# Batch 1's loads in another order, an earlier gate, and seven filler products in the opening of a Fourier-plus-channel-mix kernel

## The chip, the cores and the metric

The kernel runs on one core of one Trainium2 chip. The metric is device time in microseconds (us) of one execution. Three runs of the kernel before took 435.13, 437.23 and 437.72 us; the median is 437.23.

## The reference

```python
X = np.fft.fft(x, axis=1); X = np.fft.fft(X, axis=2); x = X.real   # x: (8, 3072, 256)
x_prev = concat([zeros, x[:, :-1, :]], axis=1)
xk = mu_k * x + (1 - mu_k) * x_prev
xr = mu_r * x + (1 - mu_r) * x_prev
k = np.maximum(xk @ w_k, 0)          # 256 -> 1024
v = (k * k) @ w_v                    # 1024 -> 256
out = sigmoid(xr @ w_r) * v
```

Eight batches of 3072 rows of 256 numbers go through the real part of a two-dimensional Fourier transform, then through a channel mix with a shift by one row.

## The kernel before, in words

The Fourier transform is a chain of small matrix products per batch. `load_xh(b, h)` loads one half (h = 0 or 1) of batch b: rows in order into `xp` (`load_p`, a plain DMA), and mirrored rows into `xm` (`load_m`, an indirect DMA over an index list; for half 0 also a small one, `load_m0`). `fold` (VectorE, L168 and L170) adds the two. The a stage (`a_sum`, `a_item`, L574 and others) multiplies by a cosine and sine table into PSUM, from where it is copied to the tile `a`; the d stage (`d_units`, L596, evicted by `d_evac` at L511 or L513) gives `g_all`; the c stage (`c_sums`, L637) gives `y`. `diff` and the mixes on VectorE turn `y` into the shifted mixes `x_t[b, 0, m]` (for w_k) and `x_t[b, 1, m]` (for w_r), where m is one of the two halves of the sequence.

The channel mix works on 48 chunks of 512 rows, three to each half of a batch. A chunk has four steps; at each step `k_piece` makes two 128-column groups of x times w_k (L748), which ScalarE evicts with a Relu (L758) and VectorE or ScalarE squares (L768, L766). `r_item` (L775, evicted with a Sigmoid at L780) makes the gate r. `v_part` (L801) and `v_tile` (L789) multiply the squares by w_v into two PSUM buffers, and `v_out` (VectorE, L811) multiplies by r and stores the rows with DMAs from the SP queue.

All instructions are in a fixed order on each engine (`pin_order`), the order in which the program writes them: an opening written out by hand, up to the first products with w_k, and then a table of steps (`at`, `event`). A blocked instruction blocks everything behind it on its engine. For instance `at(4, fold, 1, 0)` puts the fold of batch 1, half 0 into VectorE's order at step 4, ahead of that step's square.

All loads of x and of the weights w_k, w_r and w_v go through POOL's queue, in its order. POOL uses eight completion semaphores in turn, so each of its DMAs is issued only when the one eight before it has landed. `load_gate` holds POOL back until VectorE has reached a given place: VectorE clears a one-element tile with a memset (L451), and POOL writes the same tile with an iota (L452), which must wait for that. `loads_1` opens with this gate and then gathers w_r for the first half of the channel mix (`wr_sb[0]`) and loads both halves of batch 1. `loads_2`, at step 4 of the table, makes new index lists and gathers w_k and w_r for the second half (`wk_sb[1]`, `wr_sb[1]`).

`keep_busy(n, ps, cols)` (L203) puts n products of a tile of zeros into TensorE's order; nothing reads their result. The tuple `NF` holds the counts for places in the opening. `NF[0]`, nine products into the PSUM tile `fill`, stands ahead of the small products for the mu columns (L834 and L330); `NF[3]`, three, ahead of the first d stage.

Of the kernel before, what the change touches and what calls it, by code (L numbers as in the profile page):

```python
# [20 lines left out]
def _v(ap, extra_offset, free_dims):  # L21
    new_ap = [list(ap.ap[0])] + [[s, c] for (s, c) in free_dims]
    return dataclasses.replace(ap, offset=ap.offset + extra_offset, ap=new_ap)
# [16 lines left out]
def kernel(  # L40
# [37 lines left out]
    def ps_w():  # L78
        return ps_slot("W", 3, 1024)

    def ps_v():
        return ps_slot("V", 2, 512)
# [35 lines left out]
    def x_tiles(b, h):  # L118
        xp_t[b, h] = xp_sb[(2 * b + h - 1) % 3] if b or h else xp_00
        xm_t[b, h] = xm_sb[(2 * b + h) % 3]  # L120
# [3 lines left out]
    def parts(b):  # L124
        return 112 if b > 1 else 96

    def load_p(b, h):
        r, n = 9 * h, 9 - h
        if b > 1:
            for g in range(2):  # L130
                src = dataclasses.replace(x[b, 32 * g + r:32 * g + r + 1, :],
                                          ap=[[64 * D, N1], [D, n], [1, D]])
                nc.gpsimd.dma_start(out=xp_t[b, h][64 * g:64 * g + N1, 0:n], in_=src)
            return
        src = dataclasses.replace(x[b, r:r + 1, :], ap=[[32 * D, 96], [D, n], [1, D]])
        nc.gpsimd.dma_start(out=xp_t[b, h][0:96, 0:n], in_=src)

    def gather(dst, src, idx):
        nc.gpsimd.indirect_dma_start(dst, None, src, bass.IndirectOffsetOnAxis(ap=idx, axis=0))  # L139

    def load_m(b, h, o, n, idx):
        gather(xm_t[b, h][0:parts(b), XM0 + o:XM0 + o + 256 * n],
               x.rearrange("b (s r) d -> (b s) (r d)", r=n), idx)

    def load_m0(b):
        if b == 0:
            gather(xm_00[:, 1:257], x.rearrange("b s d -> (b s) d"), idx_0[:, 0:1])
        else:
            load_m(b, 0, 2048, 1, (idx_g0 if b > 1 else idx_0)[:, b:b + 1])

    def load_xh(b, h):
        x_tiles(b, h)
        load_p(b, h)
        if h == 0:
            load_m0(b)
        load_m(b, h, 0, 8, (idx_g8 if b > 1 else idx_8)[:, b, h:h + 1])

    def fold(b, h, q0=0, n=0):

        n = n or 9 - h  # L160
        if (b, h) not in p_t:
            p_t[b, h] = p_pool.tile([112, 9, 256], FP16, name="p")
        k = parts(b)
        p, xp, xm = p_t[b, h][0:k], xp_t[b, h][0:k], xm_t[b, h][0:k]
        o = XM0 + 256 * (8 - h - q0)
        if (b, h, q0) == (0, 0, 0):
            xm, o = xm_00, 1
        V.tensor_tensor(out=p[:, q0:q0 + n], in0=xp[:, q0:q0 + n],  # L168
                        in1=_v(xm, o + 256, [(-256, n), (-1, 256)]), op=ALU.add)
        V.tensor_tensor(out=p[:, q0:q0 + n, 0], in0=xp[:, q0:q0 + n, 0],  # L170
                        in1=_v(xm, o, [(-256, n)]), op=ALU.add)
# [28 lines left out]
    def keep_busy(n, ps, cols=512):  # L200

        for _ in range(n):
            nc.tensor.matmul(out=ps[:, 0:cols], lhsT=zeros,  # L203
                             rhs=_v(zeros, 0, [(0, cols // P), (1, P)]), start=True, stop=True)

    fill = ps_w()
    keep_busy(4, fill)
    NF = (9, 0, 0, 3, 0, 3, 0)


    mu_row = const.tile([2, 256], FP32)
# [49 lines left out]
    def ts(out, in0, s1, op0, s2=None, op1=None):  # L261
        kw = {} if op1 is None else {"op1": op1}
        V.tensor_scalar(out=out, in0=in0, scalar1=s1, scalar2=s2, op0=op0, **kw)
# [17 lines left out]
    def rv(n, o, *dims, k=1):  # L281
        return _v(rw_0[0:k], P * n + o, list(dims)) if n < 6 else _v(rw_1, P * (n - 6) + o, list(dims))
# [45 lines left out]
    def outer(out, *pairs):  # L328
        for n, (row, r) in enumerate(pairs):
            nc.tensor.matmul(out=out, lhsT=row, rhs=r, start=n == 0, stop=n == len(pairs) - 1)  # L330
# [45 lines left out]
    ang_ps = [ps_v(), ps_v()]  # L376
# [31 lines left out]
    ts(ueo, ueo, TURN - 1, ALU.bitwise_and)  # L408
    keep_busy(NF[0], fill)

# [12 lines left out]
    def rows():  # L423
        for a in range(2):
            for half in range(2):
                iota(_v(row_i[64 * half:64 * half + 64], a, [(3 - 2 * a, 2)]), pattern=[[0, 2]],
                     base=256 * a + half * (1 - 2 * a), channel_multiplier=2 - 4 * a)
        iota(row_i[0:1, 2:3], pattern=[[0, 1]], base=0, channel_multiplier=0)
        iota(_v(row_i[0:1], 1, [(2, 2)]), pattern=[[0, 2]], base=128, channel_multiplier=0)
# [11 lines left out]
    def loads():  # L441
        rows()
        for a in range(2):
            gather(wk_sb[0][a], moe_w_k, row_i[:, a:a + 1])
        nc.gpsimd.dma_start(out=wv_sb, in_=moe_w_v.rearrange("(fc p) v -> p fc v", p=128))
# [4 lines left out]
    def load_gate():  # L450
        V.memset(gate, 0)  # L451
        iota(gate, pattern=[[0, 1]], base=0, channel_multiplier=0)  # L452

    def loads_1():
        load_gate()
        for a in range(2):
            gather(wr_sb[0][a], moe_w_r, row_i[:, a:a + 1])
        load_xh(1, 0)
        load_xh(1, 1)

    def loads_2():
        for lo in (0, 64):
            k = slice(lo, 64 if lo == 0 else 112)
            iota(idx_g8[k], pattern=[[S // 8, B], [-1, 2]], base=S // 8 - 1 - lo // 16,
                 channel_multiplier=-8)
            iota(idx_g0[k], pattern=[[S, B]], base=S - lo // 2, channel_multiplier=-64)
        iota(idx_g0[0:1], pattern=[[S, B]], base=0, channel_multiplier=0)
        for a in range(2):
            gather(wk_sb[1][a], moe_w_k, row_i[:, 2 + a:3 + a])
        for a in range(2):  # L470
            gather(wr_sb[1][a], moe_w_r, row_i[:, 2 + a:3 + a])

# [42 lines left out]
    def a_tile(b):  # L515
        a_t[b] = y_pool.tile([P, 2, NU, 64], FP16, name="a")
# [45 lines left out]
    def a_sum(b, h, i0, eng="A", m=4):  # L562


        if (h, i0) == (0, 0):
            a_tile(b)
        ps = ps_w() if m == 4 else ps_v()
        for i in range(m):
            parts = [(h, i0 + i + 1 - h, 0, 2 * WA, 0, 1)]
            if h and i0 + i == 7:  # L570
                parts = [(0, 0, 0, WA, WA, 1), (1, 7, 1, WA, 1, 2)]
            for half, q, o, n, w, step in parts:
                for k in range(2):
                    nc.tensor.matmul(out=_v(ps, 256 * i + o, [(2 * WA // n, n)]),  # L574
                                     lhsT=p_t[b, half][0:96, q, 128 * k:128 * k + 128],
                                     rhs=_v(w_pm[0:96], (WA + WB) * k + w,
                                            [(WA + WB, 2), (step, n // 2)]),
                                     start=(k == 0), stop=(k == 1))
        a_ps[b, h, i0] = ps
        if eng:  # L580
            a_evac(b, h, i0, eng, m)
# [3 lines left out]
    def a_evac(b, h, i0, eng, m=4):  # L585
        evac(_v(a_t[b], 8 * h + i0, [(16, 2 * WA), (1, m)]),
             _v(a_ps[b, h, i0], 0, [(1, 2 * WA), (256, m)]), eng)
# [12 lines left out]
    def d_evac(ps, u0, n, bank, eng):  # L600
        evac(_v(g_all, 256 * u0, [(64, 2), (128, 2 * n), (1, 64)]),
             _v(ps, 0, [(bank, 2), (64, 2 * n), (1, 64)]), eng)
# [234 lines left out]
        outer(mu_ps[:, 4 + n:5 + n], (tv(TO + n, 0, (1, P)), rv(ONE, 0, (1, 1))))  # L837
    for k in range(2):
        outer(mu_ps[:, 64 + NU * k:64 + NU * k + NU], (rw_h[:, k], rv(JR, 0, (1, NU))))
    a_sum(0, 0, 0)  # L840
    fold(0, 0, 5, 4)
    a_sum(0, 0, 4)
    half_tables(mu_ps)
    V.tensor_copy(out=muf_t, in_=mu_ps[:, 0:6])
    loads()
    fold(0, 1, 0, 4)
    a_sum(0, 1, 0, "A")
    fold(0, 1, 4, 4)
# [8 lines left out]
    fill = ps_w()  # L857
    keep_busy(NF[3], fill)
    small = [ps_v(), ps_v()]
# [14 lines left out]
    turned(2, 4, small[1][:, 256:258], "V")  # L874
    d_evac(fill[:, 256:1024], 4, 1, 512, "A")
    d_evac(fill[:, 384:1024], 5, 1, 512, "V")
    x_t[0, 0, 0] = mix_pool.tile([P, 2, 1536], FP16, name="x00")
    for a in range(2):
        t = x_t["t", a] = mix_pool.tile([P, 24, 64], FP16, name=f"t{a}")
# [3 lines left out]
    for a in range(2):  # L883
        for z in range(2):
# [2 lines left out]
                                   scalar=mu_f[:, a, 0:1],  # L887
                                   in1=_v(x_t["t", a], 64 * z, [(128, 2), (1, 64)]),
                                   op0=ALU.mult, op1=ALU.add)
    loads_1()  # L890
    y, odd = y_t[0], ps_v()
    even = ps_v()
    for f in range(2):
        c_sums((w[:, 0:512], w[:, 512:1024]), 5, 4, f)
    keep_busy(NF[5], w[:, 768:1024], 256)
    turned(4, 8, fill[:, 0:4])
    c_sums((even, odd), 9, 8, 0)
    keep_busy(NF[6], w[:, 768:1024], 256)
    c_sums((even, odd), 9, 8, 1)
# [217 lines left out]
```

## Time and profile before

| | before |
|---|---|
| median of three runs | 437.23 us (435.13 to 437.72) |
| the profiled execution's own time | 439.32 us |
| its span, first to last instruction | 437.2 us |
| TensorE busy | 425.7 us (97%) |
| VectorE busy | 361.5 us (83%) |
| ScalarE busy | 321.6 us (74%) |
| POOL busy | 63.8 us (15%) |
| mean granted TensorE clock | 0.992 |
| read from and written to memory | 32.08 MB and 25.17 MB |

Times in the profile count from the start of the span. PE is TensorE's products, PEld its weight loads, DVE VectorE, ACT ScalarE, POOL GpSimd. A line such as L801 is the line in the kernel before. The clock row (PEclk) gives the granted share of TensorE's full clock. Busy shares are means over the whole span; the opening, about the first 40 us, looks different from the rest, and has to be read by its own timeline.

### The profile page before, as it was taken

How to read it: one execution, taken by the hardware profiler on the slowest of the kernel's cores; microseconds unless marked ns; L12 is line 12 of the kernel's file. 1: busy time of each engine (PE TensorE's matmuls, PEld its weight loads, DVE VectorE, ACT ScalarE, POOL GpSimd, SP SyncE). 2: the span in 40 equal slices, each digit the busy share in tenths (PEclk: the TensorE clock that was granted, in tenths of full speed). 3: DMA queues.
4: the chain of work that ended last, by engine and by line, in shares of the span. 5: the costliest groups of instructions: out<-in, count | busy, mean ns of one | idle time of the engine just before them, and what ended most of it. 6: DMA issues, size and time to landing. Idle time of an engine off the chain costs nothing.

```text
span 437.2 us, 9304 instructions
## 1 busy us (share of the span) xinstructions
PE 425.7 (97%) x3853; PEld 299.7 (69%) x3853; DVE 361.5 (83%) x560; ACT 321.6 (74%) x375; POOL 63.8 (15%) x89
## 2 busy tenths in 40 slices
PE   8897999999999999999999999999999999999996
PEld 3564776777677777677767767776777776767675
DVE  8769889988898988989799888989889847997543
ACT  7695888787877777786787778777777867666661
POOL 7288401000041000500014000410000000000000
PEclk9898999999999999999999999999999999999999
DMA  7889953633259222863339332682322323233333
GB/s 133 118 132 194 202 99 58 120 73 73 49 111 190 60 56 68 143 148 69 71 58 189 94 73 62 111 189 50 70 63 64 70 53 72 52 71 73 73 73 97
DMA packets 34990, 41.81 MB, mean 96 GB/s; under 512 B 4098, under 2 KB 31076, under 8 KB 34948
## 3 DMA queue, kind: packets, MB, share of 16 engines
q1 hardware_dynamic: 27380, 24.92, 23.4%
q0 software_dynamic: 7264, 16.04, 22.6%
q8 instruction: 30, 0.49, 0.5%
q10 hardware_dynamic: 304, 0.26, 0.2%
q14 instruction: 12, 0.10, 0.1%
HBM read 32.08 MB, written 25.17 MB: 131 GB/s over the span
## 4 chain that ended last, share of the span: by engine, by line
PE 91%; DMA 3%; DVE 2%; POOL 1%; issue 1%; ACT 0%; DVEq 0%; ACTq 0%
PE psW L748 37%; PE psV L789 36%; PE psW L775 9%; DMA xm<-in_x_dram,idx 3%; PE psW L596 2%; PE psV L801 2%; PE psW L669 1%; PE psW L556 1%; PE psW L574 1%; PE psW L637 0%; DVE p L168 0%; POOL xm L139 0%; POOL wr L139 0%; PE psV L574 0%; DVE k L768 0%
## 5 line engine op out<-in xcount | busy, mean ns | idle before, releaser
L758 ACT ACTIVATE rl<-psW 128x1024 f16<-128x1024 f32 x192 | 195.3, 1025 | 95.7 <-PE psW L748 91.9
L748 PE MATMUL psW<-x,wk 128*128 128x512 f16 (+1 forms) x776 | 196.3, 378 | 0.5
L789 PE MATMUL psV<-wv_sb,k 128*128 128x256 f16 x1424 | 184.1, 273 | 0.0
L789 PEld LDWEIGHTS <-k 128*128 128x128 f16 x1424 | 136.9, 98 | 35.7
L768 DVE TENSOR_TENSOR k<-rl 128x2048 f16<-128x2048 f16 (+1 forms) x101 | 116.2, 1151 | 33.5 <-ACT rl L758 33.0
L748 PEld LDWEIGHTS <-wk 128*128 128x128 f16 x776 | 75.1, 98 | 54.0 <-issue 1.8
L811 DVE SCALAR_TENSOR_TENSOR o<-psV,r 128x512 f32<-128x512 f32 (+1 forms) x97 | 65.7, 680 | 16.0 <-PE psV L789 13.5
L713 DVE TENSOR_TENSOR x<-y,t 128x1536 f16<-128x1536 f16 (+2 forms) x72 | 61.6, 860 | 2.1
L775 PE MATMUL psW<-wr,x 128*128 128x256 f16 x384 | 49.8, 273 | 0.0
L780 ACT ACTIVATE r<-psW 128x1024 f16<-128x1024 f32 x48 | 48.9, 1019 | 0.8 <-PE psW L775 0.8
L775 PEld LDWEIGHTS <-x 128*128 128x128 f16 x384 | 37.5, 98 | 14.3 <-issue 0.2
L452 POOL IOTA gate<- 1x1 int32 x6 | 2.1, 356 | 205.1 <-DVE gate L451 205.1
L513 ACT ACTIVATE a<-psW 128x832 f16<-128x832 f32 x31 | 26.1, 863 | 3.2 <-PE psW L574 1.8
L139 POOL DMA_INDIRECT xm<-in_x_dram,idx_g x18 | 26.2, 1455 | 5.5 <-issue 5.2
L513 ACT ACTIVATE g_all<-psW 128x1024 f16<-128x1024 f32 (+5 forms) x37 | 25.6, 695 | 0.4 <-PE psW L619 0.2
L168 DVE TENSOR_TENSOR p<-xp,xm 112x2304 f16<-112x2304 f16 (+5 forms) x19 | 21.0, 1106 | 4.7 <-DMA xm<-in_x_dram,idx 4.7
L702 DVE TENSOR_SCALAR t<-d,muf_t 128x1536 f16<-128x1536 f16 (+2 forms) x40 | 20.7, 528 | 0.0
L702 DVE TENSOR_SCALAR t<-d,mu_m 128x1536 f16<-128x1536 f16 x32 | 19.6, 613 | 0.0
L801 PE MATMUL psV<-wv_sb,k 128*128 128x256 f16 x112 | 15.7, 283 | 3.0 <-DVE o L811 3.0
L596 PEld LDWEIGHTS <-a 128*128 128x128 f16 x208 | 14.1, 98 | 6.4 <-issue 0.4
L179 DVE TENSOR_TENSOR eo<-p 112x1152 f16<-112x1152 f16 (+3 forms) x28 | 17.8, 678 | 0.0
L513 ACT ACTIVATE pq<-psW 128x1024 f16<-128x1024 f32 (+1 forms) x18 | 15.2, 879 | 2.3 <-PE psW L669 2.3
(138 smaller groups left out, 221.3 us busy)
## 6 DMA issues: line engine op xcount, KB each, us to landing
out_dram<-o SPq DMA_DIRECT2D x189, 128.0 KB, 2.4
xp<-in_x_dram POOLq DMA_DIRECT2D x12, 216.0 KB, 4.6
xp<-in_x_dram POOLq DMA_DIRECT2D x12, 192.0 KB, 7.1
xp<-in_x_dram POOLq DMA_DIRECT2D x2, 432.0 KB, 5.2
xp<-in_x_dram POOLq DMA_DIRECT2D x2, 384.0 KB, 7.2
wv_sb<-in_moe_w_v_dram POOLq DMA_DIRECT2D x1, 512.0 KB, 8.2
xm<-in_x_dram,idx_g POOLq DMA_INDIRECT x18, 8.0
out_dram<-o ACTq DMA_DIRECT2D x1, 128.0 KB, 2.9
```

The source lines that it names most:

```text
L139: nc.gpsimd.indirect_dma_start(dst, None, src, bass.IndirectOffsetOnAxis(ap=idx, axis=0))
L513: nc.scalar.activation(out=out_ap, in_=in_ap, func=AF.Copy)
L702: V.tensor_scalar(out=dst, in0=src, scalar1=mu, scalar2=None, op0=ALU.mult)
L713: V.tensor_tensor(out=_v(x_t[b, j, m], o, [(64 * step, hi - lo), (step, 64)]), in0=y_t[b][:, lo + 3 * m:hi + 3 * m, a], in1=x_t["t", a][:, ...
L748: nc.tensor.matmul(out=st["k", ds][:, 512 * hs + lo:512 * hs + hi], lhsT=wk_sb[m][a][:, 128 * fc:128 * fc + 128], rhs=xk[:, a, 512 * i + l ...
L758: nc.scalar.activation(out=st["rl"][:, 2 * ds:2 * ds + 2], in_=st["k", ds].rearrange("p (f t) -> p f t", f=2), func=AF.Relu, bias=0.0, sca ...
L768: V.tensor_tensor(out=k2_t[c][:, lo:hi], in0=r, in1=r, op=ALU.mult)
L775: nc.tensor.matmul(out=ps[:, 256 * tb:256 * tb + 256], lhsT=x_t[b, 1, m][:, a, 512 * i + 128 * tb: 512 * i + 128 * tb + 128], rhs=wr_sb[m] ...
L780: nc.scalar.activation(out=st["r", c], in_=ps, func=AF.Sigmoid)
L789: nc.tensor.matmul(out=st["v", tb - h][:, 256 * h:256 * h + 256], lhsT=k2_t[c][:, fc, 128 * tb:128 * tb + 128], rhs=wv_sb[:, fc], start=(f ...
L801: nc.tensor.matmul(out=st["v", tb - h][:, 256 * h:256 * h + 256], lhsT=k2_t[c][:, fc, 128 * tb:128 * tb + 128], rhs=wv_sb[:, fc], start=fc ...
L811: V.scalar_tensor_tensor(out=o.rearrange("p a b -> p (a b)")[:, 0:256 * n], in0=st["v", t0][:, 0:256 * n], scalar=16.0, in1=st["r", c][:, ...
```

## The change

Three edits. The gate and the loads behind it (`loads_1`) are called ahead of the first four mixes (L885) instead of after them. In `loads_1` batch 1's first half is loaded ahead of the two w_r gathers instead of after them; the load of its second half goes to `loads_2`, between the w_k and the w_r gathers of the second half of the channel mix. And `NF[1]` and `NF[2]`, which were zero and had no place in the program, become three products into `fill` ahead of the first `a_sum` and four into the second angle tile (`ang_ps[1]`, a PSUM tile whose last reader ran earlier) ahead of the first `a_sum` of half 1.

```diff
-    NF = (9, 0, 0, 3, 0, 3, 0)
+    NF = (9, 3, 4, 3, 0, 3, 0)
...
     def loads_1():
         load_gate()
+        load_xh(1, 0)
         for a in range(2):
             gather(wr_sb[0][a], moe_w_r, row_i[:, a:a + 1])
-        load_xh(1, 0)
-        load_xh(1, 1)
...
         for a in range(2):
             gather(wk_sb[1][a], moe_w_k, row_i[:, 2 + a:3 + a])
+        load_xh(1, 1)
         for a in range(2):
             gather(wr_sb[1][a], moe_w_r, row_i[:, 2 + a:3 + a])
...
     for k in range(2):
         outer(mu_ps[:, 64 + NU * k:64 + NU * k + NU], (rw_h[:, k], rv(JR, 0, (1, NU))))
+    keep_busy(NF[1], fill)
     a_sum(0, 0, 0)
...
     loads()
+    keep_busy(NF[2], ang_ps[1])
     fold(0, 1, 0, 4)
     a_sum(0, 1, 0, "A")
...
     d_evac(fill[:, 384:1024], 5, 1, 512, "V")
+    loads_1()
     x_t[0, 0, 0] = mix_pool.tile([P, 2, 1536], FP16, name="x00")
...
-    loads_1()
     y, odd = y_t[0], ps_v()
```

## The prediction

> **What bounds the kernel now.** I read the page first, then the chain of waits of the first 80 us, then each engine's timeline there, and last the granted clock in short windows.
>
> ```profile
> span 437.2 us, 9304 instructions
> PE 425.7 (97%) x3853; PEld 299.7 (69%) x3853; DVE 361.5 (83%) x560; ACT 321.6 (74%) x375; POOL 63.8 (15%) x89
> ...
> PEclk9898999999999999999999999999999999999999
> ```
>
> TensorE is busy for 425.7 of 437.2 us; its 11.5 us of gaps lie in the first 39 us and in the last 4. From 39 us to 433 us it hardly stops (100.00 busy of each 100 us between 100 and 400). So time won ahead of 40 us reaches the end, as long as nothing behind it comes late. In the second slice (11 to 22 us) and in the fourth (33 to 44 us) the clock row dips to 8. The chain shows what stands ahead of the later dip:
>
> ```profile
> 21.68 0.98 POOL wr L139
> 22.97 0.99 POOL wr L139
> ...
> 26.21 6.44 DMA xm<-in_x_dram,idx
> ...
> 32.77 1.37 DVE p L168
> ...
> 38.33 1.87 PE psV L801 x8
> 40.19 1.43 PE psW L748 x4
> 41.62 0.87 PE psV L801 x8
> ```
>
> Columns: start, length on the chain, what. Batch 1's big mirrored load (xm) is issued at 26.21, behind the gate (21.39) and both wr gathers, and lands at 32.65. VectorE has been waiting for it since 29.06 (3.71 us), because the fold at step 4 stands ahead of everything else in its order. The late VectorE then evicts o (L811) late, and TensorE's L801, which needs that PSUM tile, stands idle from 35.28 to 38.33: 3.05 us. Its eight products then take 1.87 us and the next four L748 1.43 us, where the same groups take 0.87 and 0.86 a little later.
>
> ```profile
> 10.35 1.68 PE L574 MATMUL psW<-w_pm,p 96*128 96x208 f16 x16 [0.71 <-DVE p L170]
> 13.49 1.22 PE L574 MATMUL psW<-w_pm,p 96*128 96x208 f16 x8 [1.47 <-DVE p L170]
> 14.59 1.91 PE L574 MATMUL psV<-w_pm,p 96*128 96x208 f16 x10
> 16.22 1.39 PE L203 MATMUL psW<-zeros 128*128 128x512 f16 x3
> 17.45 0.39 PE L596 MATMUL psV<-w_eo,a 128*128 128x128 f16 x4
> ```
>
> In brackets: the idle time before the group and what ended it. These 0.71 and 1.47 us are the stretches that get fillers.
>
> ```profile
> core 0: us, PE busy (x) PEld busy (x) DVE busy (x) ACT busy (x) POOL busy (x), PEclk, DMA share, GB/s
> 10.49:13.90 3.41, 1.95 (x21) 1.56 (x20) 2.36 (x11) 2.45 (x6) 3.11 (x3) 1.00 0.94 149
> 13.90:17.30 3.40, 3.40 (x19) 2.29 (x17) 2.23 (x10) 1.50 (x3) 0.07 (x1) 0.50 0.92 119
> 34.38:37.79 3.41, 0.90 (x5) 0.29 (x3) 3.38 (x11) 2.90 (x3) 2.96 (x4) 1.00 1.05 184
> 37.79:41.20 3.41, 2.88 (x11) 1.61 (x11) 3.41 (x12) 0.00 (x0) 2.94 (x2) 0.50 1.01 156
> ```
>
> Behind each of the two thin stretches (TensorE busy 1.95 and 0.90 of 3.41 us) the granted clock is 0.50 for just 3.4 us. A stretch with 2.69 busy of 3.42 (7.07 to 10.49) had no such sequel.
>
> **The moved load.** The gate's memset (0.06 us) now stands behind the last g_all eviction, which ends at 19.84, and ahead of the four L885 mixes, which wait until 20.17 for ScalarE anyway: it costs VectorE nothing there. Without that cover it would cost 0.06. The gate's iota on POOL then ends at about 20.1 instead of 21.5. Next in POOL's order come xp, the small xm and the big xm, which were third to fifth. From xp's issue to the big xm's landing it took 32.65 - 23.97 = 8.68 us; in the opening, xp at 1.26 and the big xm landing 6.5 us after its issue at 2.81 make 8.05, with less traffic ahead. So it lands at 28.2 to 28.8. VectorE is ready at 29.06: the wait of 3.71 goes to nothing.
>
> What is late next? With 3.7 us back, VectorE reaches L811 at about 33.9. It then waits for r, whose activation ends at 34.00 (ScalarE's 1.28 us table load stands ahead of it), and for step 6's products, half done at 33.9. One eviction of 0.67 us ends near 34.7, the second at 35.3. TensorE reaches L801 at 35.28 and needs the first. I take 0.2 us of wait as left, between 0 and 0.5. So 2.85 of 3.05 us go, and with them the thin stretch: the half-clock excess of (1.87 - 0.87) + (1.43 - 0.86) = 1.57 us. Sum of this part: 4.4 us.
>
> **What is moved past what.** wr is now issued after the big xm, at about 23.9 and 25.2 instead of 21.68 and 22.97. The first to read it is r_item of step 5, on TensorE at 30.44, with the c sums (L637), L801 of step 5 and everything after queued behind it. Alone, wr landed 2.7 and 2.8 us after issue; behind the big load in the same queue it follows that landing by some 0.75 us (256 rows of 512 bytes, at the 350 such packets a us that the trace has for the wv load near 18 us): 29.0 to 29.6. Slack about 0.8, price zero; from above, the slowest wr of this trace (5.9 us to landing) gives 31.1 and a wait of 0.7. The second load of batch 1 (xp, xm of half 1) goes behind the wk gathers of the second mix, and is issued at about 29 to 32 instead of 27.43 to 29.87. With the wk bytes (512 KB at near 190 KB/us) ahead it lands near 36 to 38 instead of 36.4; its fold starts at 48.31 on VectorE, and some 5 us earlier after the change: slack 5 us. wk itself comes earlier (it landed at 37.6 and 38.9; needed at step 12, 49.13). wr of the second mix and the loads of batch 2 keep their order and move with POOL, some 1.4 us earlier. POOL's DMAs each wait for the one eight before; in the new order those have landed by then (the wv load, at 21.2, is awaited by an issue at 29). All this I cost at nothing.
>
> **The fillers.** One 512-column product at full clock is near 0.22 us (nine in 2.60 us, part of these slow, bound it from above at 0.29; the three at half clock took 1.39, 0.46 each). Three take 0.65 to 0.87 of the 0.71 us ahead of 10.35: between no cost and 0.16. Four take 0.9 to 1.2 of the 1.47 us ahead of 13.49: no cost; were the clock low already, 1.84, a cost of 0.4. Their targets' last readers on ScalarE ended by 7.6, and neither tile is read again before TensorE writes it anew, so no wait comes with them. Idle time between 10.49 and 13.90 falls from 1.47 to about 0.6 us, what the stretch before it had without a sequel.
>
> If the dip goes, sixteen products in 1.68 us say 0.097 each for L574's spacing. The eight from 13.49 then end near 14.4, the ten after the fold at 14.53 near 15.6 instead of 16.50, VectorE's cast (0.59) at 16.3 instead of 17.13, and the three fillers of NF[3] take 0.65 and are done ahead of it. L596 starts at 16.3 instead of 17.45: 1.2 us, of this execution. The load's gate moves with it, so the first part keeps its slack.
>
> [...]
>
> **Sum.** In the profiled execution 4.4 + 1.2 = 5.6 us: span 437.2 to 431.6, own time 439.32 to 433.7. The median of the timed runs, 437.23, lies 2.1 below the profiled one, and the runs span 2.6 us; a typical run may lack the first dip, since the 0.50 stretches are whole windows of 3.41 us that need not fall alike each time. So I count half of the 1.2: 437.23 - 4.4 - 0.6 = 432.2.
>
> **Rivals.**
> Fillers without effect: the first dip stays, or is not there in typical runs. For it: the profiled time is above all three timed runs. Against it: the clock rows. Gain 4.4: 432.8.
>
> The load comes later than I think. For it: POOL's indirect issues took 0.98 to 1.23 us in that stretch, but 3.34 at 39.25, and the moved ones now run beside VectorE's mixes. [...] With one such issue the landing is 2.1 us later, TensorE's slack of 0.6 is used up, about 1.5 us of wait stay, and a half-clock stretch of some 1.5 may stay too: gain 1.4 to 2.9, 434.3 to 435.8.
>
> The wait moves to wr. r_item of step 5 stands in TensorE's order ahead of all the rest, so if wr lands late the kernel has a new gap at 30.4 in place of that at 35.3. For it: its bytes now stand behind 864 KB of one load. The slowest landing of this stretch (8.1 us) puts it at 33.3: 2.9 us of wait and a dip of 1.57 again, 4.5 in all, which eats the gain; it is slower than before from a landing of 8.2 us after the issue on. At 10 us: 439. Against it: the queue ahead of wr ends with a load that VectorE has by 28.8.
>
> **How the numbers follow.** Forecast 0.53, fillers without effect 0.15, later load 0.24, wait moved to wr 0.08. Faster by over 1% (under 432.9; about 1% is what a measurement of this kernel can tell from no change): most of the first case and half of the second, 0.55. Within 1%: the rest of these and the later load, 0.38. Slower: nearly all of the last, 0.07. Range: the best case is both dips gone from the median run and no wait left, 437.23 - 4.6 - 1.2 - 0.6 for chance differences between runs = 430.8; at the top it takes in the later load and stops short of the wr case: 436.4.
>
> **What would show it.** Right: xm's wait on VectorE (3.71) under 0.5; no TensorE gap over 0.5 between 28 and 45; L801 of step 7 in 0.9 us; PEclk at 9 in the second and fourth slices; the 1.47 gap down to 0.6. Wrong: a wait of L775 for the wr DMA near 30; L801 still released by L811 after more than 1 us; a clock of 0.50 behind 13.9 in spite of the fillers; or new gaps after 45 us, where ScalarE or VectorE would have used up the time.

## The result and the profile after

The changed kernel takes 434.01 us (median of 16 runs, 432.81 to 435.0) against 437.43 for the kernel before in as many: a ratio of 0.9921, 95% interval 0.9902 to 0.9939, so 0.8% faster. Its profiled execution took 433.70 us, with a span of 431.6. In a second comparison it came to 434.30 us and a ratio of 0.9940 (0.9914 to 0.9965). Of the 110 executions of the kernel before that ran beside the experiments, four that took over 1.5% longer than its fastest are left out of the ratios and of the 106 counted below.

From the page of the changed kernel: the span, and the clock row, which has no dip left.

```profile
span 431.6 us, 9318 instructions
...
PEclk9999999999999999999999999999999999999999
```

TensorE's timeline in the opening (start, length, line, idle time ahead in brackets):

```profile
6.09 3.86 PE L203 MATMUL psW<-zeros 128*128 128x512 f16 x9
...
10.52 0.82 PE L203 MATMUL psW<-zeros 128*128 128x512 f16 x3
11.18 1.59 PE L574 MATMUL psW<-w_pm,p 96*128 96x208 f16 x16
12.61 1.03 PE L203 MATMUL psV<-zeros 128*128 128x512 f16 x4
13.47 0.88 PE L574 MATMUL psW<-w_pm,p 96*128 96x208 f16 x8
14.57 1.06 PE L574 MATMUL psV<-w_pm,p 96*128 96x208 f16 x10 [0.22 <-DVE p L170]
...
16.41 0.38 PE L596 MATMUL psV<-w_eo,a 128*128 128x128 f16 x4
```

The brackets of 0.71 and 1.47 us are gone. The nine old fillers took 3.86 us instead of 2.60 here; the first record of full clock begins at 9.62 us in this execution and at 7.07 in before's. The small products behind them end near 10.6, and the three new fillers run on to the first L574 group, which stands 0.83 us later than before. The second group is where it was (13.47 against 13.49). Its fold ended at 13.16, 0.28 us earlier than before, and it is the four fillers that fill the time to 13.47. That costs nothing, as the third group needs a fold that waits for its load until 13.62 in this execution and 13.63 before. L596 is 1.04 us earlier, at 16.41 instead of 17.45.

VectorE's and TensorE's timeline around the old gap, first before:

```profile
32.77 1.35 DVE L168 TENSOR_TENSOR p<-xp,xm 96x2304 f16<-96x2304 f16 x1 [3.71 <-DMA xm<-in_x_dram,idx]
...
38.33 1.87 PE L801 MATMUL psV<-wv_sb,k 128*128 128x256 f16 x8 [3.05 <-DVE o L811]
```

and in the changed kernel, VectorE, then TensorE:

```profile
27.95 1.35 DVE L168 TENSOR_TENSOR p<-xp,xm 96x2304 f16<-96x2304 f16 x1
...
33.05 1.29 DVE L811 SCALAR_TENSOR_TENSOR o<-psV,r 128x512 f32<-128x512 f32 x2 [0.22 <-ACT r L780]
```

```profile
29.40 1.04 PE L775 MATMUL psW<-wr,x 128*128 128x256 f16 x8
...
33.21 1.03 PE L748 MATMUL psW<-x,wk 128*128 128x512 f16 x4
34.08 1.04 PE L801 MATMUL psV<-wv_sb,k 128*128 128x256 f16 x8
```

The fold of batch 1 starts without a wait; VectorE now waits 0.22 us for r instead of 3.71 for a load. L801 follows its predecessor at once, and r_item's products have no bracket: w_r landed 3.2 us after its issue at 23.85, 2.3 us ahead of L775. The same four windows as before:

```profile
10.49:13.90 3.41, 3.41 (x32) 2.56 (x29) 2.38 (x11) 1.95 (x5) 3.10 (x3) 1.00 0.93 148
13.90:17.30 3.40, 3.05 (x35) 2.22 (x32) 2.81 (x12) 2.48 (x8) 0.08 (x1) 1.00 0.83 114
34.38:37.79 3.41, 3.41 (x26) 2.29 (x25) 3.38 (x11) 3.35 (x4) 2.63 (x3) 1.00 1.10 172
37.79:41.20 3.41, 3.41 (x29) 2.62 (x27) 3.38 (x8) 3.41 (x5) 1.49 (x2) 1.00 1.09 240
```

In its third number TensorE is busy nearly throughout, and the granted clock (the column of 1.00) never falls.

### The profile page after: what moved, and what is told of

The parts are those of the page before. It is cut to its first block, busy times and chain, and to the rows that moved or that the text cites. A ratio compares the mean times of both kernels' runs of the same rounds, so it can differ in the third digit from the quotient of the medians.

```text
span 431.6 us, 9318 instructions
## 1 busy us (share of the span) xinstructions
PE 425.1 (98%) x3860; PEld 299.3 (69%) x3860; DVE 361.4 (84%) x560; ACT 321.5 (74%) x375; POOL 59.2 (14%) x89
## 4 chain that ended last, share of the span: by engine, by line
PE 94%; ACT 2%; DMA 1%; POOL 1%; DVE 1%; issue 1%; ACTq 0%; POOLq 0%
PE psW L748 38%; PE psV L789 36%; PE psW L775 10%; PE psV L801 3%; PE psW L596 2%; PE psW L669 1%; PE psW L556 1%; DMA xm<-in_x_dram,idx 1%; ACT rl L758 1%; POOL xm L139 1%; PE psW L637 1%; PE psW L574 0%; ACT g_all L513 0%; DVE x L888 0%; PE psV L574 0%
## 5 line engine op out<-in xcount | busy, mean ns | idle before, releaser
L789 PE MATMUL psV<-wv_sb,k 128*128 128x256 f16 x1424 | 184.1, 273 | 0.0
L811 DVE SCALAR_TENSOR_TENSOR o<-psV,r 128x512 f32<-128x512 f32 (+1 forms) x97 | 65.9, 681 | 15.5 <-PE psV L789 13.4
L775 PE MATMUL psW<-wr,x 128*128 128x256 f16 x384 | 49.8, 273 | 0.0
L775 PEld LDWEIGHTS <-x 128*128 128x128 f16 x384 | 37.5, 98 | 14.3 <-issue 0.2
L139 POOL DMA_INDIRECT xm<-in_x_dram,idx_g x18 | 23.1, 1285 | 5.5 <-issue 5.2
L596 PEld LDWEIGHTS <-a 128*128 128x128 f16 x208 | 14.0, 98 | 6.6 <-ACT mu_n L857 0.6
L690 DVE TENSOR_TENSOR d<-y 128x1664 f16<-128x1664 f16 (+5 forms) x19 | 16.7, 879 | 0.0
```

The costliest lines, as they stand in the source:

```text
L596: nc.tensor.matmul(out=ps[:, o:o + 128], lhsT=a_t[b][:, e, 2 * (u0 + i):2 * (u0 + i) + 2, :], rhs=w_eo[:, e], start=True, stop=True)
L775: nc.tensor.matmul(out=ps[:, 256 * tb:256 * tb + 256], lhsT=x_t[b, 1, m][:, a, 512 * i + 128 * tb: 512 * i + 128 * tb + 128], rhs=wr_sb[m] ...
L789: nc.tensor.matmul(out=st["v", tb - h][:, 256 * h:256 * h + 256], lhsT=k2_t[c][:, fc, 128 * tb:128 * tb + 128], rhs=wv_sb[:, fc], start=(f ...
L811: V.scalar_tensor_tensor(out=o.rearrange("p a b -> p (a b)")[:, 0:256 * n], in0=st["v", t0][:, 0:256 * n], scalar=16.0, in1=st["r", c][:, ...
```

## The experiments

Theory: the time came from three places, the gap ahead of L801, the half-clock windows behind it and behind the opening's thin stretch, and what the fillers win in the opening. Rivals: the fillers do nothing; the gate and the order each do it alone, or only together; w_r becomes the next to be late. Each run also gives its mean granted clock, which sorts the executions: one window of 3.41 us at half lowers the mean by 0.004 (3.41 / 2 of some 435 us), and 0.998 or more is taken to mean that none was lost ahead of the end (the clock falls once more behind the last products, which end at 433.09 us in before's profile, with a record of half clock from 437.15; that this can take up to 0.002 is an estimate, as no run has a mean between 0.996 and 0.998). "At full clock" below means 0.998 or more.

| kernel | ratio to before (95%) | median | at full clock: runs, median |
|---|---|---|---|
| before, beside e1 to e12 | | 437.82 (106 runs) | 28 of 106, 435.44 |
| changed | 0.9921 (0.9902 to 0.9939) | 434.01 | 16 of 16, 434.01 |
| changed, again (e5) | 0.9940 (0.9914 to 0.9965) | 434.30 | 12 of 12, 434.30 |
| fillers only (e1) | 0.9968 (0.9942 to 0.9994) | 436.06 | 9 of 12, 435.93 |
| loads only (e2) | 0.9942 (0.9911 to 0.9972) | 435.28 | 4 of 12, 433.94 |
| gate only (e3) | 0.9947 (0.9915 to 0.9979) | 436.00 | 4 of 12, 434.07 |
| order only (e4) | 0.9932 (0.9900 to 0.9965) | 434.26 | 7 of 12, 433.26 |
| order, all fillers (e6) | 0.9926 (0.9903 to 0.9950) | 434.02 | 12 of 12, 434.02 |
| order, second fillers (e7) | 0.9929 (0.9908 to 0.9950) | 434.23 | 12 of 12, 434.23 |
| changed, second fillers (e8) | 0.9952 (0.9924 to 0.9979) | 434.74 | 10 of 12, 434.60 |
| order, six and four (e9) | 0.9930 (0.9900 to 0.9960) | 435.35 | 2 of 12, 433.9 |
| w_r late (e10) | 1.0073 (1.0036 to 1.0109) | 441.46 | 0 of 10 |
| changed, first fillers (e12) | 0.9958 (0.9930 to 0.9986) | 435.64 | 6 of 12, 434.98 |

The kernel before came to 438.32 us beside e1 to e4, 437.50 beside e5 to e8, 438.40 beside e9 to e11 and 437.34 beside e12. These four sets of runs stand on three chips (e1 to e4, e5 to e11, e12). The share of before's executions that lost a window is alike on them (24 of 33, 41 of 56, 13 of 17), but a comparison across the sets, such as e12 with e5, is less direct than one within a set.

### Fillers only

```diff
-    NF = (9, 0, 0, 3, 0, 3, 0)
+    NF = (9, 3, 4, 3, 0, 3, 0)
+    keep_busy(NF[1], fill)          # ahead of a_sum(0, 0, 0)
+    keep_busy(NF[2], ang_ps[1])     # ahead of fold(0, 1, 0, 4)
```

> The seven fillers alone, gate and loads as before. Theory (the dip behind 13.9 us is the sequel of the thin stretch ahead of it): clock full from 10.5 to 35 us, L596 starts 1.0 to 1.2 us earlier than before (near 16.4 instead of 17.45), but the TensorE gap of about 3 us ahead of L801 and a half-clock window behind it stay, only earlier. Span about 436.1 against 437.2 in the profile; timed median 0.5 to 1.2 us below before. Rival (the fillers bring nothing; what before loses at 13.9 has another cause): clock 0.50 there all the same, median within 0.4 us of before.

The median is 436.06 us, 2.3 below before's beside it; by the ratio (0.3%) it is 1.4. Both are more than the 0.5 to 1.2 expected. The timeline of TensorE:

```profile
36.17 1.20 PE L801 MATMUL psV<-wv_sb,k 128*128 128x256 f16 x8 [1.94 <-DVE o L811]
```

Its granted clock by windows, cut where the clock records cut them:

```profile
11.52:14.93 3.41, 2.63 (x23) 1.66 (x20) 2.31 (x11) 2.72 (x6) 2.06 (x3) 1.00 0.91 127
14.93:18.35 3.42, 3.15 (x39) 2.25 (x38) 2.73 (x12) 2.34 (x7) 0.00 (x0) 1.00 1.00 130
32.00:35.41 3.41, 2.23 (x15) 1.26 (x13) 3.37 (x11) 3.26 (x5) 2.80 (x3) 1.00 1.07 200
35.41:38.83 3.42, 2.66 (x20) 1.85 (x20) 3.42 (x11) 1.53 (x2) 2.94 (x4) 1.00 1.15 147
```

No dip in the opening, as the theory has it. The gap is still there but measures 1.94 us, not 3.05, and no half-clock window follows it. The executions at full clock show the other side: 435.93 against 435.44 for before. The fillers win nothing there; they raise the share of such executions from 28 of 106 to 9 of 12. The rival falls by the clock rows; for the time, the interval (0.06 to 0.6%, 0.3 to 2.5 us) just reaches its 0.4 us. For an execution that had no dip anyway it holds.

### Loads only, gate only, order only

```diff
     def loads_1():                  # loads only and order only
         load_gate()
+        load_xh(1, 0)
...                                  # w_r gathers
-        load_xh(1, 0)
-        load_xh(1, 1)               # to loads_2, behind wk_sb[1]
```

```diff
+    loads_1()                       # loads only and gate only
     x_t[0, 0, 0] = mix_pool.tile([P, 2, 1536], FP16, name="x00")
...
-    loads_1()                       # behind the L885 mixes
```

> The earlier gate and the new load order, without the fillers. Theory: VectorE's wait for batch 1's load (3.7 us) and TensorE's gap (3.05) both under 0.5 us, no half-clock window after 30 us; the one behind 13.9 us may stay. Timed median 2.5 to 4.4 us below before, 0 to 1.2 above the kernel with both edits. Rival (load and fillers only work together, as the earlier clock is what makes the load early enough): a gap of over 1 us ahead of L801, gain under 2 us.

> Only the gate moved ahead of the first mixes; load order as before, no fillers. Theory: all of the loads 1.4 us earlier, so the big xm lands 1.4 us earlier, VectorE's wait falls from 3.7 to 2.3 us, TensorE's gap from 3.05 to about 1.7, perhaps still with a half-clock window behind it. Timed median 1.0 to 2.9 us below before. Rival (the load is bound by bytes that are still in the queue, not by its issue): landing less than 0.5 us earlier, gain under 0.5.

> Only the load order changed; gate after the mixes as before, no fillers. Theory: the big xm is issued 2.3 us earlier and lands 2.3 us earlier, near 30.3; VectorE waits 1.3 us, TensorE's gap falls to 0.6 to 0.8 and its half-clock window goes. Timed median 2.3 to 4 us below before. Rival (w_r is the next to be late): L775 of step 5 waits for the w_r gather, which is issued near 25 to 27 and lands near 30 to 31, a new gap of up to 1 us at 30.4, gain under 2.

By the medians the three are 3.0, 2.3 and 4.1 us below before, within or beside what the theory gave. The gate alone leaves a wait; gate only, first VectorE, then TensorE:

```profile
31.96 1.35 DVE L168 TENSOR_TENSOR p<-xp,xm 96x2304 f16<-96x2304 f16 x1 [1.03 <-DMA xm<-in_x_dram,idx]
```

```profile
37.51 1.20 PE L801 MATMUL psV<-wv_sb,k 128*128 128x256 f16 x8 [0.36 <-DVE o L811]
```

Only 0.36 us of gap is seen, but TensorE was itself late here, by two half-clock windows in the opening. Order only leaves no wait, where 1.3 us on VectorE and 0.6 to 0.8 on TensorE were expected. VectorE's fold comes without a bracket, and TensorE has no gap ahead of L801:

```profile
29.75 1.37 DVE L168 TENSOR_TENSOR p<-xp,xm 96x2304 f16<-96x2304 f16 x1
```

In these profiles the order of the loads frees VectorE by itself, and the earlier gate alone does not quite. That the order is worth more in time is likely but not shown, as the intervals of order only and gate only overlap. What loads only lacks against the changed kernel is the clock: 8 of its 12 executions lost a window or more, with a median of 435.63 against 433.94 for the other four. The rival that load and fillers only work together falls.

### The changed kernel again, and other companions for the order

> The changed kernel itself once more, as the reference point of the next three on the same chip. Median near 434.0 us, 3 to 4 below before, nearly every execution at a granted clock of 0.998 or more.

As expected: 434.30 us, every execution at full clock.

```diff
-    NF = (9, 3, 4, 3, 0, 3, 0)      # e6: all seven, gate left behind the mixes
+    NF = (9, 0, 4, 3, 0, 3, 0)      # e7: as e6; e8: with the earlier gate
```

> New load order and all seven fillers, but the gate left behind the first mixes. Theory (order alone already frees VectorE at step 4, the earlier gate adds nothing once the order is right): median within 0.6 us of the changed kernel, 433.3 to 434.3, no executions with a lowered clock. Rival (the gate is needed as soon as the fillers pull the opening forward): VectorE waits over 0.7 us for batch 1's load and the median lies over 0.8 us above the changed kernel.

> New load order, gate behind the first mixes, and only the four fillers of the second stretch. Theory (the three fillers of the first stretch cost up to 0.8 us where the clock is still low, and it is the 1.47 us stretch that lowers the clock): executions at full clock some 0.3 to 0.8 us faster than with all seven, near 433.2, and still few with a lowered clock: median 433.2 to 433.8. Rival (both stretches count together for the clock): a third or more of the executions at 0.996 or below, median above 434.3.

> The changed kernel without the three fillers of the first stretch. Theory: 0.3 to 0.8 us faster at full clock than the changed kernel, few executions with a lowered clock, median 433.3 to 433.9. Rival (both stretches count): a third or more at 0.996 or below, median at 434.5 or above.

e6 agrees with the theory: without the earlier gate the kernel is as fast (434.02 and 434.30, overlapping intervals), and no execution has a lowered clock. In e7 and e8 the clock stays up with the four fillers alone, but for 2 of 12 in e8. The second half of that expectation is wrong: leaving out the first three wins nothing (434.23 and 434.74 where 433.2 to 433.9 was expected).

### The counter-check on the fillers

```diff
-    NF = (9, 3, 4, 3, 0, 3, 0)
+    NF = (9, 3, 0, 3, 0, 3, 0)      # changed kernel without the second four
```

> The changed kernel without the four fillers of the second stretch (the first stretch keeps its three). Theory (the clock goes down for the 1.47 us stretch ahead of L574, so the four are the ones that count): a third or more of the executions at a granted clock of 0.996 or less, as without any fillers (8 of 12), median 434.8 to 435.5. Rival (it is the busy share of whole windows, to which either group adds enough): at most 2 of 12 at 0.996 or less, median 434.0 to 434.6.

Half of the executions lose a window, and the median is 435.64, so the four of the second stretch count and the rival falls. The windows of this run, cut where the clock records cut them, hold the second stretch but not the first:

```profile
12.09:15.50 3.41, 1.89 (x21) 1.45 (x19) 2.41 (x10) 3.00 (x7) 1.79 (x2) 1.00 0.86 123
15.50:18.92 3.42, 3.42 (x27) 2.45 (x26) 1.57 (x5) 1.33 (x4) 0.00 (x0) 0.50 1.17 163
```

```diff
-    NF = (9, 0, 4, 3, 0, 3, 0)
+    NF = (6, 0, 4, 3, 0, 3, 0)      # e9: as e7, with six instead of nine
```

> New load order, gate behind the first mixes, four fillers in the second stretch, and six instead of nine ahead of the mu products (the nine took 2.5 to 3.9 us, depending on when the clock comes up, and at 3.9 they hold up what stands behind them). Theory (at full clock the opening is set by the first loads' landing and by these fillers): executions at full clock 0.2 to 0.7 us faster than with nine, median 433.3 to 434.0. Rival (fewer fillers leave the window ahead too thin, and the clock comes up a window later or drops again): executions at 0.996 or below, median over 434.5.

The rival came true: 10 of 12 executions at 0.996 or less, against 0 of 12 in e7 on the same chip. With three old fillers fewer TensorE is busy for 2.04 of 3.41 us in the window ahead of the first L574 group, the next window is at half, and that group, which starts at 10.34, takes 2.80 us instead of 1.68 in e7:

```profile
7.14:10.55 3.41, 2.04 (x16) 1.15 (x14) 3.31 (x13) 2.75 (x4) 2.72 (x9) 1.00 1.05 197
10.55:13.96 3.41, 3.41 (x19) 2.54 (x17) 2.87 (x13) 1.72 (x4) 3.10 (x3) 0.50 0.87 137
```

### w_r made late

```diff
         load_gate()
         load_xh(1, 0)
-        for a in range(2):
-            gather(wr_sb[0][a], moe_w_r, row_i[:, a:a + 1])
...
         load_xh(1, 1)               # in loads_2
+        for a in range(2):
+            gather(wr_sb[0][a], moe_w_r, row_i[:, a:a + 1])
```

> The changed kernel with the first half's w_r gathers moved further back, behind the second w_k gathers and the second load of batch 1. This is the rival of the prediction in which the wait moves to w_r, made to happen: the gathers are issued near 30.5 and 32, behind 512 and 768 KB, and land near 36 to 37.5 instead of 27. Theory (the wait is the landing minus 29.4, plus 1.6 us for a half-clock window behind it): a TensorE gap of 6.5 to 8 us ahead of L775 of step 5, and a time 8 to 10 us above the changed kernel, 442 to 444. Rival (TensorE makes part of it up, since VectorE and ScalarE run ahead in the gap): under 6 us.

```profile
34.92 1.97 PE L775 MATMUL psW<-wr,x 128*128 128x256 f16 x8 [6.09 <-DMA wr<-in_moe_w_r_dram,row_i]
```

This line of TensorE's timeline shows the gap of 6.09 us where the rival puts it; the clock is at half from 32.7 to 39.5. The gap is below the theory's 6.5 to 8. The time is 7.2 us above the changed kernel's on the same chip (434.30), less than the theory's 8 to 10 and more than the rival's 6. The mechanism is real and makes the kernel slower than before; in the changed kernel's profile it has 2.3 us of slack.

### The kernel before, a second profile

> The kernel before, for a second profile. Theory (the 3.05 us gap of the first profile was on the large side, since the load took 8.7 us from its first issue to VectorE's fold where it takes 7.6 with the fillers alone or the gate alone): the gap ahead of L801 is 1.5 to 2.5 us here. Rival: 2.8 us or more again, and the difference to the timed median has another cause.

The code is before's, without an edit. VectorE's fold, then TensorE's L801:

```profile
34.34 1.35 DVE L168 TENSOR_TENSOR p<-xp,xm 96x2304 f16<-96x2304 f16 x1 [3.37 <-DMA xm<-in_x_dram,idx]
```

```profile
39.89 1.19 PE L801 MATMUL psV<-wv_sb,k 128*128 128x256 f16 x8 [2.71 <-DVE o L811]
```

2.71 us lies between the two expectations. With 1.94 and 3.05 it says that the gap is no constant: the same load, issued in the same order, keeps VectorE waiting 2.61, 3.37 or 3.71 us. This execution took 441.29 us, with two half-clock windows in the opening and one behind the gap.

## Why the prediction was right or wrong

The mechanism and the profiled execution are right. The sum said span 431.6 and own time 433.7; the changed kernel's profile has 431.6 and 433.70. The load's wait and the gap went, r became the next thing VectorE waits for (34.0 foreseen, less the 1.0 that the opening won), no half-clock window was left, L596 starts at 16.41 where 16.3 was worked out, and w_r was in time. By the starts of L801 (38.33 and then 41.46 before, 34.08 and 35.81 after) the opening brought 1.04 us where 1.2 was forecast, and the gap and the half-clock window together 4.61 where 4.4 was forecast, because no wait was left ahead of L801. The two misses cancel, so the exact agreement is in part luck; executions of one kernel also differ by over 2 us.

The later load did not come: the two xm issues took 0.96 and 0.93 us beside VectorE's mixes. A long issue does occur, but on a later load (3.26 us on wk in e5's profile), where nothing waited for it.

The measured median, 434.01, lies in the range, but 1.8 us above the forecast of 432.2, and the likeliest class, faster by over 1%, did not come: it is 0.8%. The step that failed is "437.23 - 4.4 - 0.6 = 432.2". It took the whole 4.4 us of the load from one profile and held it against the median of other executions. The mechanism was right and a term was too large, the gap's. Term by term:

- The gap was put at 2.85 us won. At full clock before and after differ by 435.44 - 434.01 = 1.4 us (1.1 by the second comparison). The one profile of the old load order without any dip (fillers only) has a gap of 1.94. The 3.05 of the first profile is the longest of the three seen. The executions of before at full clock may be those with the shorter gaps, so 1.4 need not be the typical one.
- The half-clock window behind the gap was put at 1.57 us, as if every execution had it. Fillers only, which has the gap but hardly a dip in the opening, has a lowered clock in 3 of 12.
- The opening was put at 1.2 us in the profile and half of it in the median. Here the guess that a typical run may lack the dip was the wrong way round: loads only, which has only the opening's dips, shows them in 8 of 12, and before in 78 of 106 from either cause. The cost of the dips from both causes is the larger part of the gain: before's median less its median at full clock is 437.82 - 435.44 = 2.4 us. The sum had 1.57 + 0.6 = 2.2 us for the two, so the clock's share was about right in all, and the opening has more of it than was forecast.

The four fillers keep the clock up, though the gap that they fill was only 1.47 us in before's profile (order only has 5 of 12 lowered, with the four, e7, 0 of 12; the changed kernel 0 of 28 in its two comparisons, without the four, e12, 6 of 12). "Fillers without effect" was right in one respect only, for executions at full clock. "Three take 0.65 to 0.87 us ... between no cost and 0.16" missed that the nine ahead of them may take 3.86. Then no idle time is left for the three, and they put the first group 0.83 us late; a load that comes later still hid it.

Two things stay open. Executions of the changed kernel differ by up to 3 us at full clock (433.28 to 436.29 in e5), so something besides the clock varies. The profiles show two parts of it. The first loads land at different times: L596 starts at 16.41 us in the changed kernel's first profile and at 15.64 in e5's. And there is a stall for which the prediction has no term: VectorE's L811 waits for an earlier store of o to land. With the new load order that wait is 0.93 us in the changed kernel's first profile, 0.85 in order only, 0.19 in e5, 0.66 in e6 and 0.91 in e9; with the old order none of the four profiles has it up to 46 us. In the first profile TensorE does not feel it. It reaches TensorE in e12, where L811 waits 1.96 us until 45.91 and L801 then has a gap of 1.17, and in e5, the changed kernel's second profile (VectorE, then TensorE):

```profile
52.22 0.69 DVE L811 SCALAR_TENSOR_TENSOR o<-psV,r 128x512 f32<-128x512 f32 x1 [1.27 <-DMA out_dram<-o]
...
54.70 0.27 PE L596 MATMUL psW<-w_eo,a 128*128 128x128 f16 x2 [0.60 <-DVE g_all L511]
```

Between 30 and 60 us a store lands 7.7 us after its issue (median) in the changed kernel's first profile and 9.1 in e5's, against 4.0 to 5.8 in the four profiles with the old order. So a new gap behind 45 us, one of the prediction's signs of being wrong, does occur, though not in the first profile. That the earlier loads hold up the stores is a guess; no run tests it, no profile was taken of a slow execution at full clock, and how much of the missing 1.8 us it makes is not known.

The second open point: order only reaches 433.26 at full clock, 0.7 less than with the earlier gate, on one chip and in few runs; on the other chip the two gate positions with all fillers do not differ. None of the versions is clearly faster than the changed kernel.

## What to carry to other kernels

A cost read from one profile belongs to that execution: where a stall ends with a transfer (2.61 to 3.71 us for one load here), or a clock window decides (78 of before's 106 executions lost at least one), look at the spread of the runs (time and mean clock of each) before setting the term against a median. Put the load that blocks a strictly ordered engine ahead of loads that are needed later; here that alone ended the wait, where issuing all of them earlier left 1.03 us of it. Then look at what runs beside the moved loads, such as the stores. The filler products paid here by keeping windows at full clock, in 9 of 12 executions instead of 28 of 106 with nothing else changed; at full clock they won nothing (435.93 against 435.44).

## What the runs showed of the hardware

The granted clock changes in windows of 3.41 us: before's clock records are 6.83, 3.41, 20.48, 3.41 and 395.95 us long, up to its last, and the first of the changed kernel's is 423.25, all whole multiples of 3.413. The windows lie differently in the two executions, as the first record of full clock begins at 7.07 us in one and at 9.62 in the other. Lined up with the clock records, the full-clock windows with TensorE busy for 0.57 and 0.26 of it (before, from 10.49 and 34.38), 0.49 (gate only, from 10.40), 0.38 (order only, from 11.63) and 0.55 (e12, from 12.09) were each followed by a window at half. Those at 0.79 (before, from 7.07) and at 0.77 and 0.65 (fillers only, from 11.52 and 32.00) were followed by full clock. At 0.60 one was followed by half (e9, above) and one was not, loads only:

```profile
12.68:16.09 3.41, 2.06 (x21) 1.68 (x21) 2.64 (x11) 3.00 (x8) 1.17 (x2) 1.00 0.89 148
16.09:19.50 3.41, 3.08 (x43) 2.13 (x41) 2.65 (x10) 2.29 (x6) 0.12 (x2) 1.00 1.19 149
```

The idle time in a window that was followed by half is as little as 1.37 us (e9, 3.41 - 2.04) and 1.46 (before, 3.41 - 1.95). The busy share of one window is not all that counts: at the end of the changed kernel's profile the window from 426.05 is busy for only 0.46, and the next is at full clock all the same:

```profile
426.05:429.46 3.41, 1.57 (x14) 1.04 (x11) 1.33 (x3) 0.00 (x0) 0.00 (x0) 1.00 0.76 197
429.46:432.87 3.41, 0.00 (x0) 0.00 (x0) 0.00 (x0) 0.00 (x0) 0.00 (x0) 1.00 0.11 31
```

A window at half is not always followed by one at full. Gate only lost two in a row, though TensorE was busy for 3.14 of 3.41 us in the first:

```profile
10.40:13.82 3.42, 1.68 (x16) 1.30 (x16) 2.76 (x11) 1.86 (x4) 3.05 (x3) 1.00 0.92 154
13.82:17.23 3.41, 3.14 (x19) 2.83 (x20) 1.91 (x10) 2.29 (x7) 0.27 (x1) 0.50 0.93 126
17.23:20.64 3.41, 3.41 (x26) 2.35 (x24) 1.61 (x7) 1.04 (x3) 0.00 (x0) 0.50 0.94 128
```

The busy share does not explain this: before's window at half from 37.79, busy for only 2.88 of 3.41 us, was followed by full clock. What decides it stays open.

By before's runs a lost window goes with 1.9 us the first time and 1.6 the second: 435.44 at full clock, 437.34 at a mean clock of 0.994 to 0.996, 438.97 at 0.990 to 0.993. Half of a 3.41 us window is 1.7 us, so the clock can account for all of it; but a longer gap may also go with a lost window (behind the gaps of 3.05 and 2.71 us stands a window at half, behind that of 1.94 none), and the groups were not told apart by that.
